# A second step of the seven-product scheme in the first product of strips 2 to 8

## The chip, the cores and the metric

The kernel runs on one core of a Trainium2 chip. The metric is the device time of one execution in microseconds (us). Five engines work from queues of their own: TensorE (PE in the profile, its weight loads PEld), VectorE (DVE), ScalarE (ACT), GpSimd (POOL) and SyncE (SP), which here issues nearly all transfers (DMA).

## The reference

```python
def _attn_ref(q, k, v, g_norm):                 # (8, 8, 576, 64) each, g_norm (64,)
    kv = np.einsum('bhsd,bhse->bhde', k, v)
    out = np.einsum('bhsd,bhde->bhse', q, kv)
    rms = np.sqrt(np.mean(out * out, axis=-1, keepdims=True) + 1e-06)
    return (out / rms * g_norm).astype(np.float32)

def _moe_ref(x, w_in, w_out):                   # x (4608, 512), w_in (512, 2048), w_out (2048, 512)
    h = x @ w_in
    r = np.maximum(h, 0.0)
    g = r * r
    return (g @ w_out).astype(np.float32)
```

The attention output, with heads side by side, is the x of the second part. Everything is fp32; the weights arrive as 64-bit words and are converted in the kernel.

## The kernel before

The 4608 rows of x are nine strips of 512 rows, numbered s = 0 to 8 here as in the code. Each strip has a first product (x @ w_in, then relu and square) and a second product (@ w_out). The attention work that makes the rows of later strips is cut into slices (`slices`, `attend`), and the main loop puts some of them between the steps of the products, spread over the first 42% of a strip's work. The order on each engine is the order in which the program's lines run (`tc.manual_schedule()`); the loop near the end of the function writes it by hand: a list `steps` per strip, one function call each, with other work hung on certain step numbers.

Both products save multiplications by the seven-product scheme for 2x2 blocks (seven products of half-size blocks in place of eight, at the price of sums of blocks). The order of the seven is `ORDER` = 1, 2, 6, 5, 7, 3, 4, and they accumulate in PSUM banks named by `BANK`: products 1, 6, 7, 4 follow each other in bank A, 5 and 3 in B, 2 in C. After products 1, 6 and 5 ScalarE copies the bank to SBUF (`snap`, L621); a result is a bank plus such a copy.

- **First product.** Strip 0 is plain (`up_first`). From strip 1 on, `up(s, g, p)` takes one step of the scheme: 4 groups g of columns by 7 products p, each of 2 x 2 matmuls of a 128x128 block of weights with 256 columns of x (L611). `combine` calls `relu_squared`: an add of bank and copy (L675) and a fused relu and square (L676) on VectorE; for the last result ScalarE does both from the bank (L680, L681). The results lie in four tiles `gq[s, 11], [12], [21], [22]`. The block sums of w_in are kept in SBUF (`w_in[..., 0:7]`, places by `A_IN`), those of x are made by `sums_x` on VectorE.
- **Second product.** From strip 1 on it takes two steps of the scheme: `down_deep(s, k, i)` runs seven outer products (`DEEP_ORDER`) of seven inner ones, `small_products`, each of four matmuls with 128 columns (L821). `leaf_sums` makes the inner sums of `gq` on VectorE, `together` adds the results, `send` stores them. The sums of w_out lie in DRAM (`w_out`, `w_deep`) and are streamed: `stream()` issues the next load into a pool of four 1 MB buffers (`stream_pool`), one call per half of an outer product, so that a load is asked for when the buffer's last user has been issued.
- **Buffers.** [...]`fpsum` holds four by tags (A twice, B, C); `apsum` holds two for keys, values and transposes ("at") and one tile of two banks for queries. `c_pool` has six buffers for the copies and the output tiles, `sum_pool` eight for sums.
- **Strip 0** also converts the weights and makes their sums; at its last step it calls `stream(2)`.

Of the kernel before, what the change touches and what calls it, by code (L numbers as in the profile page):

```python
# [20 lines left out]
def kernel(  # L21
# [50 lines left out]
    N_STRIP = N_TILE // NT  # L72
    DEEP = 1
    SQ = 32
    Q_ON_PE = 2
# [16 lines left out]
    wtmp = conv.enter_context(tc.tile_pool(name="wtmp", bufs=4))  # L92
    fpsum = ctx.enter_context(tc.tile_pool(name="fpsum", bufs=1, space=bass.MemoryType.PSUM))
    opening = ExitStack()
# [89 lines left out]

    w_deep = dram.tile([7, P, 4, FQ // 2, P], FP32, name="w_deep")

    w_out_11, w_out_21, w_out_t1 = w_first = [
# [280 lines left out]
    def first_features(p):  # L468
        t, x = x_n.pop(("first", p)), open_xt(0)
        ps = fpsum.tile([P, NT, P], FP32, name="xt_ps", tag="C")  # L470
        for n in range(NT):
            nc.tensor.transpose(ps[:, n, :], t[:, n, :], ident)
        nc.scalar.activation(x[:, :, p, :], flat(ps).rearrange("p (a t) -> p a t", t=SQ), AF.Copy, scale=g_col)
# [3 lines left out]
    def first_up(p, tiles):  # L477

        for j in tiles:
            if p == 0:  # L480
                first_sums[j] = fpsum.tile([P, STRIP], FP32, name=f"ps_{TAG_UP[j]}", tag=TAG_UP[j], bufs=2 if TAG_UP[j] == "A" else 1)
            fh, i = divmod(j, 2)
            nc.tensor.matmul(
                first_sums[j], lhsT=w_in[:, p % KH, 0, p // KH * 2 + fh, ts(i, P)], rhs=xt[0][:, :, p, :],
                start=p == 0, stop=p == NP - 1,
            )
# [115 lines left out]
    def open_bank(p):  # L602
        b = BANK[p]
        if p in (1, 5, 2):
            bank[b] = fpsum.tile([P, 2, 2 * P], FP32, name=f"ps_{b}", tag=b, bufs=2 if b == "A" else 1)
        return bank[b]
# [37 lines left out]
    def up_first(g, fh, i):  # L644

        tag = TAG_UP[2 * fh + i]
        if g == 0 and 2 * fh + i in first_sums:
            ps = first_sums.pop(2 * fh + i)
        else:
            ps = fpsum.tile([P, STRIP], FP32, name=f"ps_{tag}", tag=tag, bufs=2 if tag == "A" else 1)  # L650
            for kc in range(NP):
                nc.tensor.matmul(
                    ps, lhsT=w_in[:, kc % KH, g, kc // KH * 2 + fh, ts(i, P)], rhs=xt[0][:, :, kc, :],
                    start=kc == 0, stop=kc == NP - 1,
                )
        dest = quarters(0, g)
        for th in range(2):
            o = dest[(11, 12, 21, 22)[2 * fh + th]][:, i, :]
            nc.scalar.activation(o, ps[:, ts(th, TH)], AF.Relu)
            nc.scalar.activation(o, o, AF.Square)  # L660
# [24 lines left out]
    for p, t in zip((1, 2, 5), w_first):  # L685
        w_blk[0, p] = t.rearrange("p f (h e) -> p h f e", h=2)
    DEEP_ORDER = (4, 1, 2, 6, 5, 7, 3)
    to_stream = [(s, p) for s in range(DEEP) for p in ORDER if (s, p) not in w_blk]
    to_stream += [(s, p, n) for s in range(DEEP, N_STRIP) for p in DEEP_ORDER for n in range(2)]
    to_stream = iter(to_stream)  # L690
# [4 lines left out]
    def stream(n=1):  # L695
        for _, u in zip(range(n), to_stream):
            p = u[1]
            t = stream_pool.tile([P, 4, FQ // 2, P], FP32, name="w_blk", tag="w_blk")
            if len(u) == 2:
                w_blk[u] = t.rearrange("p (h a) f e -> p h (a f) e", h=2)  # L700
# [92 lines left out]

    def leaf_sums(s, p):
        a = gq[s, A_G[p]]
        a11, a12, a21, a22 = (a[:, ts(f, FQ // 2), ts(t, P)] for t in range(2) for f in range(2))
        s1, s2, s3, s4 = (sum_pool.tile([P, FQ // 2, P], FP32, name=f"g_s{i}", tag="sum") for i in range(4))
        leaf[p] = {1: a11, 2: a12, 3: s4, 4: a22, 5: s1, 6: s2, 7: s3}
        nc.vector.tensor_tensor(out=s1, in0=a21, in1=a22, op=ALU.add)
        minus(nc.vector, s2, s1, a11)  # L800
        minus(nc.vector, s4, a12, s2)
        minus(nc.vector, s3, a11, a21)


# [5 lines left out]
    def small_products(s, p, js):  # L810
        c = "B" if p in (4, 2, 5, 3) else "A"
        if js[0] == 1 and p not in (6, 7, 3):
            chain[c] = [
                fpsum.tile([P, 4, P], FP32, name=f"ps_{c}", tag=t, bufs=2 if t == "A" else 1)
                for t in ("AA" if c == "A" else "CB")
            ]
        for j in js:
# [34 lines left out]
    def down_deep(s, k, i):  # L852
# [28 lines left out]
        if k == 6 and s + 1 < N_STRIP:  # L881
            sums_x(s + 1)

    attend(ready[0])
    opening.close()
    apsum = ctx.enter_context(tc.tile_pool(name="apsum", bufs=2, space=bass.MemoryType.PSUM))
    for i in range(NP, NP + 2):
        convert_on_act(i)
    acted[0] = NP + 2
    for s in range(N_STRIP):  # L890
        attend(ready[s])
        if s == 0:
            steps = [(2, up_first, (g, fh, i)) for g in range(NG) for fh in range(2) for i in range(2)]
# [10 lines left out]
        for i, (w, fn, a) in enumerate(steps):  # L904
# [28 lines left out]
            if s:  # L933
                attend(ready[s] + int((goal - ready[s]) * min(done / (0.42 * total), 1)))
                if s >= DEEP and i == n_up - 3:
                    leaf_sums(s, 4)
                continue
            if i == n_up + 1:
# [8 lines left out]
            if i == n_up + 11:  # L947
                sums_x(1)
            if i == len(steps) - 1:
                stream(2)  # L950

            n = i + 1 - (n_up - 6)
# [35 lines left out]
```

## Time and profile before

| | |
|---|---|
| runs | 938.18, 933.09, 938.22 us (median 938.18) |
| profiled execution | span 932.3 us; the page lists no other time for it |
| granted TensorE clock | 0.995 |
| first product of strips 2 to 8, from the chain's stage boundaries | 54.6, 54.2, 54.7, 55.5, 54.7, 50.5, 48.4 us |
| second product of strips 1 to 8 | 43.8 us each |
| DMA | 191.48 MB, mean 205 GB/s, main queue 62.9% of 16 engines |

The page lists busy time by engine, the chain of work that ended last (followed back from the last instruction to whatever released it), groups of instructions by line with the mean time of one, and transfers. Matmuls overlap, so the mean duration of a matmul record (381 ns at L611, 275 ns at L821) is longer than the distance from one to the next; the distance is read from stretches of the chain. Some groups the text uses, with mean ns of one: L621 ScalarE copy of a bank, 586; L675 VectorE add, 680 to 690; L676, 692; L680 and L681 on ScalarE, 597 and 630; VectorE SBUF sums of 128x512, 683 to 692, and of 128x2048, 2284. Loads of 768 KB (`w_blk<-w_out`) land 5.1 us after issue, those of 1 MB 5.5 us. VectorE waited four times, 6.2 us at most, for a load of q, in strip 1 the longest.

### The profile page before, as it was taken

What the parts mean: (1) busy time and instruction counts of PE and PEld (TensorE: products, weight loads), DVE (VectorE), ACT (ScalarE), POOL (GpSimd) and SP (SyncE); (2) the same over time, 40 slices, a digit from 0 to 9 for tenths busy, and PEclk for the clock granted to TensorE, in tenths of its full rate; (3) what the DMA queues carried; (4) which work ended last, traced back from release to release, by engine and by line L of the source; (5) the groups of instructions that cost most, each with busy time, mean ns of one, the idle gap of its engine ahead of it and who ended that gap; (6) DMA issues with size and microseconds to landing.
All of it is one profiled execution on the core that took longest, in us unless ns stands there. A gap on an engine that the chain in (4) does not pass through costs nothing.

```text
span 932.3 us, 17478 instructions
## 1 busy us (share of the span) xinstructions
PE 913.8 (98%) x7070; PEld 810.1 (87%) x7070; DVE 684.3 (73%) x1195; ACT 225.9 (24%) x494; POOL 1.7 (0%) x7
## 2 busy tenths in 40 slices
PE   6999999999999999999999999999999999999998
PEld 6534788889988998899889998899889988998898
DVE  3899979379737985589648974797559855983496
ACT  3797432320022002310221022201230022002200
POOL 0000000000000000000000000000000000000000
PEclk8999999999999999999999999999999999999999
DMA  8599998828853685568564865477507731682075
GB/s 279 205 295 303 290 382 249 262 85 291 314 138 90 235 301 158 113 218 296 171 155 159 295 217 144 111 286 257 158 24 262 268 105 57 245 287 67 1 264 177
DMA packets 165728, 191.48 MB, mean 205 GB/s; under 512 B 84112, under 2 KB 137872, under 8 KB 157200
## 3 DMA queue, kind: packets, MB, share of 16 engines
q1 hardware_dynamic: 165328, 190.23, 62.9%
q8 instruction: 56, 0.92, 0.4%
q10 hardware_dynamic: 320, 0.13, 0.1%
q14 instruction: 24, 0.20, 0.1%
HBM read 159.12 MB, written 31.20 MB: 204 GB/s over the span
## 4 chain that ended last, share of the span: by engine, by line
PE 83%; DVE 7%; DMA 4%; ACT 2%; SPq 2%; issue 1%; DVEq 0%; ACTq 0%
PE ps_A L611 23%; PE ps_B L821 21%; PE ps_A L821 16%; PE ps_B L611 11%; PE ps_C L611 6%; PE kv_ps L366 2%; DVE w_t L249 2%; PE x_ps L397 2%; DMA w_out<-w_in 1%; DMA q<-in_q_dram 1%; DVE w_in L249 1%; ACT w_c L211 1%; DVE w_c L229 1%; DMA v_rest<-in_v_dram 1%; DVE gt L249 1%
## 5 line engine op out<-in xcount | busy, mean ns | idle before, releaser
L611 PE MATMUL ps_A<-x_t,w_in 128*128 128x256 f32 x768 | 183.3, 381 | 0.1
L611 PEld LDWEIGHTS ps_A<-x_t,w_in 128*128 128x128 f32 x768 | 144.4, 190 | 20.6 <-DVE gt L675 0.6
L821 PE MATMUL ps_B<-w_blk,g_s 128*128 128x128 f32 x1024 | 124.8, 275 | 0.0
L821 PEld LDWEIGHTS ps_B<-w_blk,g_s 128*128 128x128 f32 x1024 | 119.5, 192 | 0.0
L821 PE MATMUL ps_B<-w_blk,gt 128*128 128x128 f32 x768 | 96.2, 275 | 0.0
L821 PE MATMUL ps_A<-w_blk,g_s 128*128 128x128 f32 x768 | 93.6, 275 | 0.0
L821 PEld LDWEIGHTS ps_B<-w_blk,gt 128*128 128x128 f32 x768 | 91.5, 192 | 0.4
L821 PEld LDWEIGHTS ps_A<-w_blk,g_s 128*128 128x128 f32 x768 | 89.6, 192 | 0.0
L675 DVE TENSOR_TENSOR gt<-ps_A,snap 128x512 f32<-128x512 f32 x32 | 22.0, 688 | 71.0 <-PE ps_A L611 71.0
L821 PE MATMUL ps_A<-w_blk,gt 128*128 128x128 f32 x576 | 72.2, 275 | 0.0
L676 DVE SCALAR_TENSOR_TENSOR gt<-gt 128x512 f32<-128x512 f32 x96 | 66.4, 692 | 3.3
L675 DVE TENSOR_TENSOR gt<-ps_C,snap 128x512 f32<-128x512 f32 x32 | 22.1, 690 | 63.2 <-PE ps_C L611 63.2
L821 PEld LDWEIGHTS ps_A<-w_blk,gt 128*128 128x128 f32 x576 | 68.2, 192 | 0.0
L621 ACT COPY snap<-ps_A 128x512 f32<-128x512 f32 x66 | 38.7, 586 | 114.1 <-PE ps_A L611 103.0
L611 PE MATMUL ps_B<-xT,w_in 128*128 128x256 f32 x256 | 61.1, 381 | 0.4 <-ACT snap L621 0.4
L611 PE MATMUL ps_A<-xT,w_in 128*128 128x256 f32 x256 | 61.2, 382 | 0.0
L611 PE MATMUL ps_C<-xT,w_in 128*128 128x256 f32 x256 | 61.1, 381 | 0.0
L611 PE MATMUL ps_B<-x_t,w_in 128*128 128x256 f32 x256 | 61.0, 381 | 0.0
L249 DVE TENSOR_TENSOR gt<-gt 128x2048 f32<-128x2048 f32 (+1 forms) x29 | 59.7, 2063 | 0.0
L835 DVE TENSOR_TENSOR o_sb<-o_sb,ps_B 128x256 f32<-128x256 f32 (+1 forms) x128 | 49.4, 386 | 12.5 <-ACT o_sb L836 4.2
L611 PEld LDWEIGHTS ps_B<-xT,w_in 128*128 128x128 f32 x256 | 48.1, 190 | 7.5 <-ACT snap L621 0.8
L611 PEld LDWEIGHTS ps_B<-x_t,w_in 128*128 128x128 f32 x256 | 48.2, 190 | 6.7
(126 smaller groups left out, 1111.0 us busy)
## 6 DMA issues: line engine op xcount, KB each, us to landing
w_blk<-w_deep SPq DMA_DIRECT2D x56, 1024.0 KB, 5.5
w_blk<-w_out SPq DMA_DIRECT2D x56, 768.0 KB, 5.1
raw<-in_moe_w_in_dram SPq DMA_DIRECT2D x16, 512.0 KB, 5.7
raw<-in_moe_w_out_dram SPq DMA_DIRECT2D x16, 512.0 KB, 5.6
k<-in_k_dram SPq DMA_DIRECT2D x29, 256.0 KB, 2.9
v<-in_v_dram SPq DMA_DIRECT2D x29, 256.0 KB, 3.3
x_d<-x_q SPq DMA_DIRECT2D x27, 256.0 KB, 2.1
xT<-x_d SPq DMA_DIRECT2D x108, 64.0 KB, 2.0
```

The source lines that it names most:

```text
L211: nc.scalar.activation(c, high_f, AF.Abs)
L229: yield nc.vector.scalar_tensor_tensor(out=ci, in0=high, scalar=-(2**30), in1=ci, op0=ALU.bitwise_and, op1=ALU.bitwise_or)
L249: eng.tensor_tensor(out=out, in0=a, in1=b, op=ALU.subtract)
L366: nc.tensor.matmul(ps[ts(h, D)], lhsT=a, rhs=w, start=c == 0, stop=c == C)
L397: nc.tensor.matmul(ps[half, r, i, ts(p, D)], lhsT=q[row, half], rhs=kvd[b, p][row, row], start=True, stop=True)
L611: nc.tensor.matmul(bank[BANK[p]][:, i, :], lhsT=lhsT(k), rhs=rhs(k), start=p in (1, 5, 2) and i == 0 and k == 0, stop=k == n - 1, skip_gro ...
L621: nc.scalar.copy(snap[p], b)
L675: nc.vector.tensor_tensor(out=o, in0=b, in1=a, op=ALU.add)
L676: nc.vector.scalar_tensor_tensor(out=o, in0=o, scalar=0.0, in1=o, op0=ALU.max, op1=ALU.mult)
L821: nc.tensor.matmul(chain[c][x][:, i, :], lhsT=a[:, f, :], rhs=w[:, f, :], start=p not in (6, 7, 3) and j in ((1, 2) if place(s, p) is LAST ...
L835: add = lambda out, a, b: nc.vector.tensor_tensor(out=out, in0=a, in1=b, op=ALU.add)
```

## The change

From strip 2 on (`DEEP_UP = 2`) the first product takes two steps of the scheme as well. Seven outer products in the order `UP_SETS` have seven inner ones each. An inner one (`up_small`) is four matmuls of a 128x128 weight block with 128 columns of x, one for each 128-wide block of features. The outer products are staggered: a strip has 57 slots, and outer product n runs its inner product number i in slot 7n + 2i, so that two outer products alternate.

Inner results are added up by VectorE from PSUM into the copy's buffer, and GpSimd adds that into one or two of the `gq` units of the outer scheme. The fourth inner product of an outer one goes from the bank straight to `gq`. Relu and square move to ScalarE, on SBUF, two or four slots after the last addend (`relus`). Sums of x are on GpSimd: `sum_x` for the outer scheme and `leaf_x` for the inner one, the latter one outer product ahead, and for n = 0 at the end of the strip before in the place of `sums_x`.

The inner scheme needs seven forms of each of the seven weight sums. Three more per sum (`deep_sums_in`) are made on GpSimd during strip 1, stored to DRAM in `w_in_deep`, and streamed from strip 2 on: seven loads of 768 KB a strip, put into the order of `to_stream` ahead of the strip's other loads, one `stream()` call after inner product 3. One form is made in place in `w_in` once strip 1 no longer needs the original (`deep_differences_in`).

PSUM: one tag "f" with four banks takes the place of A, B and C; from strip 2 on it has five, and "at" one. The `stream(2)` at the end of strip 0 moves to four steps before the end of strip 1's first product. `leaf_sums(s, 4)` is split over two slots. Cut to its core:

```diff
+    DEEP_UP = 2
+    fpsum = psums.enter_context(tc.tile_pool(name="fpsum", bufs=4, space=bass.MemoryType.PSUM))
+    w_in_deep = dram.tile([7, P, 3, 2, WN // 2], FP32, name="w_in_deep")
...
+    UP_SETS = (1, 2, 6, 7, 5, 3, 4)
+    for s in range(DEEP, N_STRIP):
+        to_stream += [("in", s, p) for p in UP_SETS if s >= DEEP_UP]
+        to_stream += [(s, p, n) for p in DEEP_ORDER for n in range(2)]
...
         if k == 6 and s + 1 < N_STRIP:
-            sums_x(s + 1)
+            leaf_x(s + 1, 0)
...
+    def deep_sums_in(b):
+        t = stream_pool.tile([P, 4, FQ // 2, P], FP32, name="w_i", tag="w_blk")
+        s1, s2, s4 = (t[:, i].rearrange("p f e -> p (f e)").rearrange("p (g e) -> p g e", g=2) for i in range(3))
+        nc.gpsimd.tensor_tensor(out=s1, in0=w_half(b, 0, 1), in1=w_half(b, 1, 1), op=ALU.add)
+        minus(nc.gpsimd, s2, s1, w_half(b, 0, 0))
+        minus(nc.gpsimd, s4, w_half(b, 1, 0), s2)
+        nc.sync.dma_start(
+            out=w_in_deep[b].rearrange("p n g e -> p n (g e)"), in_=t[:, 0:3].rearrange("p n f e -> p n (f e)")
+        )
+    def deep_differences_in(b):
+        minus(nc.gpsimd, w_half(b, 0, 1), w_half(b, 0, 0), w_half(b, 0, 1))
...
+    def leaf_x(s, n):
+        x = operand_x(s, UP_SETS[n])
+        t = leaf_t[s, n] = sum_pool.tile([P, 4, TH // SQ // 2, SQ], FP32, name="x_l", tag="sum")
+        late = x[:, 4:8].rearrange("p a k t -> p k a t")
+        minus(nc.gpsimd, t[:, 0:2], late, x[:, :, 0].rearrange("p (h a) t -> p h a t", h=2))
+        minus(nc.gpsimd, t[:, 2], late[:, 1], t[:, 0])
+        minus(nc.gpsimd, t[:, 3], x[:, 0:4, 1], t[:, 2])
+    SUM_AT = {2: 5, 4: 6, 11: 7, 18: 4}
+    FINAL = {2: 11, 5: 22, 3: 12, 4: 21}
+    def up_slot(s, slot):
+        for n, p in enumerate(UP_SETS):
+            i, odd = divmod(slot - 7 * n, 2)
+            if not odd and 0 <= i < 7:
+                up_small(s, n, p, ORDER[i], slot)
+        if slot in SUM_AT:
+            sum_x(s, SUM_AT[slot])
+        n, at = divmod(slot, 7)
+        if at == 3 and n < 6:
+            leaf_x(s, n + 1)
+        for o in relus.pop(slot, ()):
+            nc.scalar.activation(o, o, AF.Relu)
+            nc.scalar.activation(o, o, AF.Square)
+    def up_small(s, n, p, j, slot):
...
+        for i in range(4):
...
+            nc.tensor.matmul(
+                ps[:, i, :], lhsT=w, rhs=rhs, start=j in (1, 2, 5) and i == 0, stop=True, skip_group_check=True
+            )
+        if j == 3:
+            stream()
+        if j in (1, 6, 5):
+            snap[n, j] = c_pool.tile([P, 4, P], FP32, name=f"snap{j}", tag="c")
+            nc.scalar.copy(snap[n, j], ps)
+            return
...
+        to = {1: [(12, None)], 2: [(11, 12)], 6: [(12, 12)], 7: [(21, 12)], 5: [(22, 21), (12, 12)], 3: [(12, 12)], 4: [(21, 21)]}[p]
+        if j == 4:
+            for q, before in to:
+                if before is None:
+                    nc.scalar.copy(unit(q), ps)
+                else:
+                    add(nc.vector, unit(q), ps, unit(before))
+        else:
+            other = snap.pop((n, {2: 1, 7: 5, 3: 6}[j]))
+            if p == 1:
+                add(nc.vector, unit(12), ps, other)
+            else:
+                add(nc.vector, other, ps, other)
+                for q, before in to:
+                    add(nc.gpsimd, unit(q), unit(before), other)
+        if p in FINAL:
+            relus.setdefault(slot + (2 if j == 4 else 4), []).append(unit(FINAL[p]))
...
+        if s == DEEP_UP:
+            while queried:
+                attend(slice_at[0] + 1)
+            psums.close()
+            fpsum = ctx.enter_context(tc.tile_pool(name="fpsum", bufs=5, space=bass.MemoryType.PSUM, reuse_waits="tile"))
+            apsum = ctx.enter_context(tc.tile_pool(name="apsum", bufs=1, space=bass.MemoryType.PSUM, reuse_waits="tile"))
+        if s >= DEEP_UP:
+            quarters(s, 0)
+            steps = [(0.5, up_slot, (s, slot)) for slot in range(57)]
...
+                if s == 1 and i < n_up and i % 3 == 2 and i < 21:
+                    deep_sums_in(i // 3)
+                if s == 1 and i == n_up - 4:
+                    stream(2)
+                if s == 1 and n_up <= i < n_up + 7:
+                    deep_differences_in(i - n_up)
+                if s >= DEEP_UP and i == 45:
+                    first_leaf = leaf_sums_of(s, 4)
+                if s >= DEEP_UP and i in (45, 47):
+                    next(first_leaf)
...
-            if i == len(steps) - 1:
-                stream(2)
```

## The prediction

> **What bounds the kernel now.** I read four views, in this order: busy time by engine, the chain that ended last, busy time by stage, and single instructions around the start of a strip. All times are us unless a row says ns.
>
> First the page's busy times.
>
> ```profile
> PE 913.8 (98%) x7070; PEld 810.1 (87%) x7070; DVE 684.3 (73%) x1195; ACT 225.9 (24%) x494; POOL 1.7 (0%) x7
> ```
>
> TensorE is busy nearly all the time, and GpSimd (POOL) does nothing. A busy TensorE need not be at its peak, so the second view is the chain that ended last, in order of time (start, length, what, number of instructions).
>
> ```profile
> 836.13 1.73 PE ps_A L611 x8
> 846.49 3.45 PE ps_A L611 x16
> 858.58 3.45 PE ps_A L611 x16
> 870.67 3.45 PE ps_A L611 x16
> 884.48 6.25 PE ps_B L821 x56
> 890.73 6.25 PE ps_A L821 x56
> ```
>
> This is the last strip, s = 8, which has no attention work in it. From 836.13 to 884.48 runs the first product (L611), 48.35, in a gapless chain of TensorE. Each fp32 matmul of the program appears as two instructions, so 112 matmuls on 256 columns are 224 instructions: 48.35 / 224 = 215.8 ns each. The second product (L821) takes 6.25 per 56 instructions on 128 columns: 111.6 ns each. Two levels of the seven-product scheme make 196 matmuls of 128 columns, 392 instructions. Third, the stages (length, then busy time and count by engine, clock, DMA share, GB/s).
>
> ```profile
> 347.90:402.00 54.10, 54.10 (x401) 46.22 (x401) 29.33 (x53) 14.28 (x31) 0.00 (x0) 1.00 0.53 143
> 402.00:445.80 43.80, 43.80 (x394) 43.80 (x393) 40.37 (x64) 3.10 (x9) 0.00 (x0) 1.00 0.78 278
> 836.10:884.50 48.40, 48.40 (x227) 42.61 (x226) 18.88 (x29) 10.72 (x18) 0.00 (x0) 1.00 0.15 46
> ```
>
> The first row is the first product of strip 3 with attention mixed in, the second its second product, the third the first product of strip 8. In all, TensorE is the limit, and VectorE and ScalarE have room in the first product.
>
> **What the Trainium skill says.** "GPSIMD Engine Reference", section 3.1 (elementwise accounting), gives a two-input fp32 add over 2048 elements 4497 ns on GpSimd and 2293 ns on VectorE. The trace has the VectorE half: 128x2048 takes 2284 ns and 128x512 about 690. It has no GpSimd add. "SBUF — State Buffer", section "Who interferes with whom": a VectorE instruction with two SBUF inputs and a GpSimd instruction that reads SBUF exclude each other for a whole instruction; with one SBUF input there is no conflict. No row here shows it. "TensorE: Matmul & The Clock Gate", section "Back-to-back issue gap", lets the gap grow with the columns plus a few ns; the trace agrees (215.8 against 111.6, a ratio of 1.93).
>
> **The change part by part.**
>
> *TensorE.* Seven strips lose 224 instructions at 215.8 ns (48.35) and gain 392 at 111.6 (43.75). I take 111.6 because L821 has the same shape; the moving operand's runs of 32 elements are already there in L611. Gain 4.60 a strip, 32.2 in all, all on the path.
>
> *VectorE.* Per strip it loses 12 pairs L675/L676 (12 x 1.38 = 16.6) and four sums of x (4 x 0.69), and gains 27 adds from PSUM (27 x 0.69 = 18.6): net -0.7. These adds have one SBUF input, so GpSimd doesn't block them.
>
> *ScalarE.* It loses 12 snapshots at 0.586 and four pairs at 0.597 + 0.630 (11.9), and gains 25 copies at 0.586 and 16 pairs at about 1.26 (34.8). Busy 14.3 + 22.9 = 37 of about 50: it fits, but not evenly (below).
>
> *GpSimd.* Per strip 25 operations over 512 elements and seven sets of three over 256, 128, 128. A quarter of 4497 is 1.12; I take 1.2 each and 1.4 a set, an estimate from that page. Six sets fall inside the product: 25 x 1.2 + 6 x 1.4 = 38.4, against 43.75. It fits at 88%. Lower bound 0.69 (VectorE's), upper 2.2, a doubling for software overhead.
>
> *Where GpSimd is late.* Between slots 29 and 38 of the 57 it gets nine adds and two sets, 13.6 in 8.9 of TensorE time. So the last outer product's set comes about when its third product wants it (slot 46). I take 0.3 a strip, 0 to 2.5.
>
> *Start of a strip.* Here only one outer product is under way. Product 6 accumulates on the bank that ScalarE copies after product 1; between them stands one product of 0.89, where there was one of 1.73. At the start of strip 8 that copy waits for an output DMA to free its buffer:
>
> ```profile
> 837.90 0.59 ACT L621 COPY snap<-ps_A 128x512 f32<-128x512 f32 x1 [2.36 <-DMA out_dram<-o_sb]
> ```
>
> The copy ends 2.36 after the strip's start, and two products cover 1.79, so 0.8 with the semaphores; there were four such waits in all. I take 0.5 a strip, 0 to 1.
>
> *End of a strip.* The last outer product has nothing beside it. Its product 4 waits for VectorE to read product 7's bank (0.69), which stands behind two leaf sums (2 x 0.69); these wait for ScalarE's pairs, and those for GpSimd's adds. One product (0.89) covers it, and the leaf sums have two SBUF inputs and can be held off by GpSimd for up to 1.2. I take 1.0, 0 to 4.
>
> *Strip 1.* 21 sums and seven differences on GpSimd, 28 x 1.2 = 34 of its 98, beside 12 L676 with two SBUF inputs and the leaf sums. TensorE waits for none of the new sums; what hides them is VectorE's slack (20 in the first product, 3.5 in the second). SP gets seven stores that wait for GpSimd, ahead of q, k and v loads; if they come late, VectorE stands at the q transpose (in this strip its longest such wait is 6.2 already). I take 1.5, 0 to 6.
>
> *DMA and SP.* 49 loads of 768 KB, 38.5 MB. The second product moves 278 GB/s at a share of 0.78, so 5.5 MB a strip are 15.5 of all engines, 0.29 of a first product: 0.53 + 0.29 = 0.82. Four buffers give each load several steps to land (5.1 in the page). Seven more issues a strip lie in SP's idle time, each behind a wait for a buffer that TensorE has just left. I cost them nothing; uncovered, a load would cost up to 5 a strip. The two loads no longer issued at the end of strip 0 come four steps before the second product of strip 1: no cost.
>
> *PSUM.* Five banks in turn for the first product, one for keys and values instead of two: these come 6.1 apart (364.18, 370.29) and their two copies take 0.42. Nothing.
>
> Sum: 932.3 - 32.2 + 7 x 1.8 + 1.5 = 914.2. The page gives the profiled execution no time apart from its span; the lowest run shown, 933.09, lies 0.8 above it, and the median, 938.18, lies 5.9 above. Against the median I add 5.9: **920**.
>
> **The rivals.**
>
> 1. *Everything is hidden.* For it: GpSimd may run ahead, since its sums of x wait only for buffers. Then 932.3 - 32.2 + 1 + 5.9 = 907.
> 2. *The queues couple.* ScalarE is in order; pairs that wait for GpSimd hold up the copies TensorE needs, and it has seven pairs (8.8) in slots 40 to 49 (8.9). At about 5 a strip the gain is gone: 932.3 - 32.2 + 35 + 1.5 + 5.9 = 942; at 3.5, 932.
> 3. *GpSimd becomes the bound*: slower. Its need is 31c + 1.2 a strip at c per add, and it idles some 6 at the strip's start, before the first results. The first products of strips 2 to 8 now last 372 together by the chain's stage boundaries, 53.2 each: from about c = 1.5 nothing is left. At c = 1.8 it is 7 x (31 x 1.8 + 1.2 + 6) = 441, so 938 + 69 = 1007. Against it: the page's price.
> 4. *The change doesn't do what it says*: the 128-column matmul is slower here than in L821. Nothing in the profile speaks for it; the operands come from the same kinds of tile.
>
> **How the numbers follow.** The likeliest case, 1 to 3 lost a strip, 912 to 929: 0.5. Rival 1: 0.2. Rival 2: 0.17. Rival 3: 0.12. Rival 4: 0.01. The range 903 to 937 takes in rival 1 and the better half of rival 2, and leaves out rival 3. About 1% (9.4) is what a measurement of this kernel can tell from no change. Faster by over 1%: 0.70; within: 0.17; slower: 0.13.
>
> **What would show it.** TensorE instructions in a first product 392 at about 111.6 ns, with L821 unchanged. A first product without attention of 45 to 47. GpSimd's 128x512 adds at 1.1 to 1.3, and 75 to 90% busy in that stage. Idle TensorE at the strip's ends, released by ScalarE's copy at the start and VectorE's add at the end. Adds of 1.5 or more, TensorE waiting for GpSimd's sums in mid-strip, or a DMA share near 1 would prove the forecast wrong.

## The result, and the profile after

The changed kernel takes 986.13 us (median of 982.77 to 990.47) against 937.4 for the kernel before: ratio 1.0533, 95% interval 1.0493 to 1.0572. It is 5% slower; 920 was forecast. The profiled execution spans 980.3 us, 48.0 more than before.

The page's busy times and its row of the granted clock, in 40 slices:

```profile
PE 909.0 (93%) x8246; PEld 843.2 (86%) x8246; DVE 724.3 (74%) x1195; ACT 361.2 (37%) x732; POOL 351.6 (36%) x357
...
PEclk7999998999999899989999999999998999999999
```

TensorE's busy time was to fall by 32.2 from 913.8 and fell by 4.8, and TensorE is now idle 71.3 instead of 18.5. So it lost some 27 of busy time that the number of instructions does not ask for, and 53 of waiting. Most of the 27 is a lower clock: the granted clock was 0.970 over the span instead of 0.995, about 25 of 980. VectorE is 40 busier with the same number of instructions. GpSimd is busy 36% of the span, and inside a first product 36.6 of 55.8 (strip 3) or 36.3 of 47.2 (strip 8).

Stages of strip 3 (first and second product) and the first product of strip 8 (length, busy time and count by engine, clock, DMA share, GB/s):

```profile
366.60:422.40 55.80, 51.33 (x571) 49.66 (x571) 35.42 (x60) 31.45 (x62) 36.57 (x38) 0.97 0.75 201
422.40:469.10 46.70, 45.82 (x394) 45.63 (x394) 37.67 (x57) 4.87 (x13) 7.74 (x9) 0.96 0.82 299
885.10:932.30 47.20, 44.67 (x395) 44.12 (x394) 24.75 (x36) 27.55 (x48) 36.31 (x37) 1.00 0.44 149
```

Without attention the first product became 1.2 shorter; with attention it became longer, and the second product, whose instructions were not touched, went from 43.8 to 46.7. By stage boundaries the 48.0 divide up like this (the last columns are two of the experiments):

| stages | before | after | both edits | all edits |
|---|---|---|---|---|
| start of strip 1 | 148.4 | 151.5 | 155.6 | 148.8 |
| strip 1, both products | 100.9 | 110.9 | 110.7 | 110.3 |
| first products of strips 2 to 6 | 273.6 | 296.8 | 266.7 | 277.4 |
| first products of strips 7 and 8 | 98.8 | 98.4 | 93.3 | 96.8 |
| second products of strips 2 to 7 | 262.6 | 274.8 | 276.9 | 263.3 |
| second product of strip 8, to the end | 48.0 | 48.1 | 50.2 | 48.6 |

The start of strip 1 varied between 147.9 and 155.6 in the profiles of kernels that share that part, so its 3.1 is no effect of the change. With the forecast's 32.2 in hand, 77 were lost: 46 in strips 2 to 6, 9 in strips 7 and 8, 12 in second products, 10 in strip 1.

What TensorE waits for (total, times, longest):

```profile
PE ps_A L972 <- DVE snap L983: 33.3, 14, 5.9
...
PE ps_B L615 <- ACT snap L625: 4.7, 1, 4.7
PE ps_A L833 <- DMA w_blk<-w_deep: 4.3, 2, 3.4
PE ps_A L972 <- POOL x_l L253: 3.7, 5, 1.3
```

The first row is TensorE waiting until VectorE has added up a finished inner product, so that its PSUM bank is free. Its place is the end of a first product: 28.2 of the 33.3 are seven stalls, one ahead of the last inner product of each of strips 2 to 8. VectorE's timeline at the end of strip 3's first product (start, length):

```profile
413.73 0.65 DVE L983 TENSOR_TENSOR snap<-ps_B,snap 128x512 f32<-128x512 f32 x1
414.31 1.42 DVE L812 TENSOR_TENSOR g_s<-gt 128x512 f32<-128x512 f32 x1
415.76 1.65 DVE L253 TENSOR_TENSOR g_s<-g_s,gt 128x512 f32<-128x512 f32 x1
417.34 0.68 DVE L983 TENSOR_TENSOR gt<-ps_A,gt 128x512 f32<-128x512 f32 x1
417.94 0.70 DVE L510 STREAM_TRANSPOSE x_q<-x_n 128x512 f32<-128x512 f32 x1
418.56 0.64 DVE L253 TENSOR_TENSOR g_s<-gt,g_s 128x512 f32<-128x512 f32 x1
419.13 0.68 DVE L253 TENSOR_TENSOR g_s<-gt 128x512 f32<-128x512 f32 x1
419.73 0.68 DVE L983 TENSOR_TENSOR snap<-ps_A,snap 128x512 f32<-128x512 f32 x1
```

TensorE stands from 416.96 to 420.56, for the last line. Four leaf sums (g_s) that the second product needs later and a transposition for the next strip stand ahead of it in the queue, and two of the four took 1.42 and 1.65 instead of 0.69, while GpSimd was at three sums in a row (412.67 to 416.87).

The second place is in the chain of waits, right after it (start, length, what):

```profile
413.96 5.41 DMA x_d<-x_q
...
421.71 4.92 DMA x_d<-x_q
...
428.49 5.59 DMA w_blk<-w_deep
...
434.12 3.84 PE ps_A L833 x32
```

Pieces of x for the next strip go through a DRAM buffer, `x_d`: SP stores a piece, stands until the store has landed, and issues the four loads that bring it back in its new layout. Here it does so twice. Only at 428.49 can it issue the load of `w_deep` that TensorE waits for until 434.12. The wait itself is 0.9 here and 3.4 in strip 4.

### The profile page after: what moved, and what is told of

It reads as the page before. It is cut to its first block, busy times and chain, and to the rows that moved or that the text cites. A ratio compares the mean times of both kernels' runs of the same rounds, so it can differ in the third digit from the quotient of the medians.

```text
span 980.3 us, 20838 instructions
## 1 busy us (share of the span) xinstructions
PE 909.0 (93%) x8246; PEld 843.2 (86%) x8246; DVE 724.3 (74%) x1195; ACT 361.2 (37%) x732; POOL 351.6 (36%) x357
## 4 chain that ended last, share of the span: by engine, by line
PE 61%; DVE 18%; DMA 8%; ACT 4%; issue 3%; POOL 3%; SPq 3%; DVEq 0%; ACTq 0%
PE ps_B L833 19%; PE ps_A L833 14%; PE ps_A L972 13%; PE ps_B L972 5%; PE ps_C L972 3%; POOL gt L983 3%; DVE g_s L253 2%; DMA x_d<-x_q 2%; PE kv_ps L370 2%; DVE w_t L253 1%; PE ps_A L615 1%; DVE snap L983 1%; DVE w_c L233 1%; DMA q<-in_q_dram 1%; DMA w_blk<-w_deep 1%
## 5 line engine op out<-in xcount | busy, mean ns | idle before, releaser
L983 POOL TENSOR_TENSOR gt<-gt,snap 128x512 f32<-128x512 f32 x147 | 187.3, 1300 | 148.5 <-DVE snap L983 135.7
L972 PE MATMUL ps_A<-x_l,w_in 128*128 128x128 f32 x784 | 110.9, 287 | 32.6 <-DVE snap L983 32.6
L972 PEld LDWEIGHTS ps_A<-x_l,w_in 128*128 128x128 f32 x784 | 99.9, 200 | 35.4 <-issue 29.3
L253 POOL TENSOR_TENSOR x_l<-xT 128x256 f32<-128x256 f32 x21 | 15.7, 750 | 245.2 <-PE ps_A L833 245.2
L979 ACT COPY snap<-ps_A 128x512 f32<-128x512 f32 x98 | 57.0, 581 | 92.2 <-PE ps_A L972 82.6
L956 ACT ACTIVATE gt<-gt 128x512 f32<-128x512 f32 x112 | 70.3, 628 | 32.2 <-POOL gt L983 32.0
L903 POOL TENSOR_TENSOR w_i<-w_in 128x512 f32<-128x512 f32 x7 | 9.2, 1308 | 176.7 <-DMA w_blk<-w_out 154.2
L957 ACT ACTIVATE gt<-gt 128x512 f32<-128x512 f32 x112 | 70.6, 630 | 3.6
L848 ACT COPY o_sb<-ps_B 128x128 f32<-128x128 f32 x32 | 8.5, 266 | 167.8 <-PE ps_B L833 167.8
L983 DVE TENSOR_TENSOR snap<-ps_A,snap 128x512 f32<-128x512 f32 x42 | 28.7, 683 | 45.3 <-PE ps_A L972 27.4
L972 PE MATMUL ps_A<-x_l,w_blk 128*128 128x128 f32 x392 | 53.3, 279 | 3.7 <-POOL x_l L253 3.7
```

The lines of the kernel that those rows point to most:

```text
L253: eng.tensor_tensor(out=out, in0=a, in1=b, op=ALU.subtract)
L848: yield nc.scalar.copy(q[:, 3:4], small(1))
L956: nc.scalar.activation(o, o, AF.Relu)
L972: nc.tensor.matmul(ps[:, i, :], lhsT=w, rhs=rhs, start=j in (1, 2, 5) and i == 0, stop=True, skip_group_check=True)
L979: nc.scalar.copy(snap[n, j], ps)
L983: add = lambda eng, out, a, b: eng.tensor_tensor(out=out, in0=a, in1=b, op=ALU.add)
```

## Experiments

Four theories were put against each other. **V**: at a strip's end VectorE's queue is the bound. **D** (later **B**): the bytes of the streamed sums make other loads late. **G**: GpSimd's sums are late. **S**: strip 1 loses its time because GpSimd and VectorE exclude each other. **Q**, on the order in SP's queue (SP stands at x_d, and loads that TensorE needs are queued behind), came after the first four runs, and **R**, its counterpart for strip 1, after the next four. "Both edits" is leaf sums late and loads late.

| run | median us | ratio to before, 95% interval |
|---|---|---|
| changed kernel | 986.13 | 1.0493 to 1.0572 |
| e1 leaf sums late | 976.42 | 1.0391 to 1.0454 |
| e2 strip 1's sums out | 985.3 | 1.0488 to 1.0540 |
| e3 a third of the bytes | 970.06 | 1.0328 to 1.0376 |
| e4 Newton step, one input | 983.93 | 1.0480 to 1.0540 |
| e5 as e2, one store | 986.33 | 1.0488 to 1.0604 |
| e6 loads of x_d late | 972.9 | 1.0351 to 1.0433 |
| e7 both edits | 951.33 | 1.0148 to 1.0210 |
| e8 both, a third of the bytes | 950.48 | 1.0138 to 1.0211 |
| e9 both, strip 1's sums out | 945.53 | 1.0066 to 1.0121 |
| e10 both, Newton step, one input | 949.57 | 1.0097 to 1.0167 |
| e11 both, strip 1 moved | 955.46 | 1.0168 to 1.0225 |
| e12 both, attention to the end | 978.12 | 1.0417 to 1.0471 |
| e13 both, attention early | 958.18 | 1.0199 to 1.0305 |
| e14 both, leaf sums between adds | 955.22 | 1.0180 to 1.0211 |
| e15 both, GpSimd's order in strip 1 | 951.38 | 1.0143 to 1.0189 |
| e16 all edits | 946.89 | 1.0096 to 1.0127 |
| e17 all, half sums | 938.3 | 1.0013 to 1.0053 |
| e18 kernel before, loads of x_d late | 936.36 | 0.9992 to 1.0018 |

**e1: leaf sums late.**

```diff
-                if s >= DEEP_UP and i == 45:
+                if s >= DEEP_UP and i == 53:
...
-                if s >= DEEP_UP and i in (45, 47):
+                if s >= DEEP_UP and i in (53, 55):
```

> The changed kernel, but the first leaf sums of strips 2 to 8 are issued to VectorE after slots 53 and 55 instead of 45 and 47, so behind product 3's add. Theory V (at the end of a first product, VectorE's queue is the bound: the leaf sums stand ahead of the last adds from PSUM that TensorE waits for, and are stretched by GpSimd): TensorE's waits for snap L983, 33 in all, fall below 12; the second product then waits 1 to 2 a strip for its own leaf sums; 15 to 20 us off the 986, so 966 to 971. Theory D (the streamed sums of W_in make other loads late) and theory G (GpSimd's sums come too late): no change, 982 to 990, because the adds are late for other reasons.

It came to 976.42, about 10 off instead of 15 to 20. TensorE's waits in this kernel:

```profile
PE ps_B L833 <- DVE g_s L253: 12.4, 9, 1.9
PE ps_A L833 <- DMA w_blk<-w_deep: 10.1, 4, 4.9
PE ps_A L972 <- DVE snap L983: 9.8, 7, 2.4
```

The wait for snap fell from 33.3 to 9.8, as V says, and the first products of strips 2 to 6 lost 22. But the second products of strips 3 and 4 rose from 46.7 and 47.9 to 54.6 and 56.3: the stall at the strip's end had been hiding a late load. A good part of the gain went to the next thing that was late.

**e2: strip 1 without GpSimd's sums.** The three sums in `deep_sums_in` and the difference in `deep_differences_in` go; three DMAs store raw parts instead of one that stores the sums.

```diff
-        nc.gpsimd.tensor_tensor(out=s1, in0=w_half(b, 0, 1), in1=w_half(b, 1, 1), op=ALU.add)
...
+        for n, (kc, f) in enumerate([(0, 1), (1, 1), (0, 0)]):
+            nc.sync.dma_start(
+                out=w_in_deep[b][:, n], in_=w_half(b, kc, f)
+            )
...
```

> The changed kernel without GpSimd's 21 sums and seven differences in strip 1; the stores to w_in_deep stay in place and copy raw parts of W_in, so the results of strips 2 to 8 are those of other weights. Theory S (strip 1 loses its 13 us to GpSimd and VectorE excluding each other): VectorE's w_in sums back at 0.69 from 1.65, strip 1's first product at 114 instead of 123 and its second at 44 instead of 47.6: 973. If it were the seven stores in SP's queue instead: no gain, 984 to 988.

985.3, no gain: a miss, but a confounded one. VectorE's last three sums of W_in were back at 2.02, and yet strip 1 took 112.9, with TensorE waiting 4.9 for `w_out` behind SP's store of x_d. The extra DMAs had lengthened SP's queue.

**e3: a third of the bytes.**

```diff
-                nc.sync.dma_start(out=w_blk[u][:, 0:3], in_=w_in_deep[A_IN[p]].rearrange("p n g e -> p n (g e)"))
+                nc.sync.dma_start(out=w_blk[u][:, 0:1], in_=w_in_deep[A_IN[p]][:, 0:1].rearrange("p n g e -> p n (g e)"))
...
```

> The changed kernel, but each load of further sums of W_in brings one of its three parts (256 KB instead of 768), which is used for all three products: the results of strips 2 to 8 are those of other weights. Theory D (the stream makes q, v, x and w_deep late): VectorE's waits for q fall from 22.7 to about 11, the two waits for w_deep (4.3) and the v waits (3.3) go, and with them lowered clocks in the second products: 15 to 25 us less, 961 to 971. Theories V and G: 3 to 6 us less, 980 to 983, since the ends of the strips stay as they are.

970.06, in D's range: late loads cost something. But the waits for snap stayed at 31.5. It doesn't say yet whether the bytes are the cause, or an order that smaller loads only mend in part: one `w_deep` wait of 3.0 was left.

**e4: the Newton step with one input.** The three operations of `inverse_root` become `tensor_scalar`, the second for example:

```diff
-        nc.vector.tensor_tensor(out=t, in0=t, in1=r, op=ALU.mult)
+        nc.vector.tensor_scalar(out=t, in0=t, scalar1=1.0, scalar2=1.0, op0=ALU.mult, op1=ALU.mult)
```

> The changed kernel, but the three small VectorE operations of the Newton step have one SBUF input each (same number, same shapes, the step itself is not computed, so the inverse root stays that of the first estimate). If GpSimd's exclusion of two-input operations matters here: they fall from 0.4 to 0.5 us to 0.17, VectorE's busy time falls by about 13, and 1 to 2.5 us come off each strip with attention (2 to 6) and 2 off strip 1: 972 to 979. If that time lies in VectorE's slack: 984 to 988.

983.93, not to be told from no change. The edit missed its aim, as the group of the second operation in this kernel shows (count, busy us, mean ns):

```profile
L423 DVE TENSOR_SCALAR newton<-newton 128x16 f32<-128x16 f32 x14 | 6.8, 484 | 0.5
```

With one SBUF input it is as long as with two (394 in the changed kernel), against 175 before. Whether the stretched small operations matter stays open.

**e5: as e2, one store a set.**

```diff
-        nc.gpsimd.tensor_tensor(out=s1, in0=w_half(b, 0, 1), in1=w_half(b, 1, 1), op=ALU.add)
...
+        nc.sync.dma_start(
+            out=w_in_deep[b].rearrange("p n g e -> p (n g) e"),
+            in_=w_in[:, :, :, b].rearrange("p k g e -> p (k g) e")[:, 0:6],
+        )
```

> As the kernel without GpSimd's 28 sums and differences in strip 1, but each store to w_in_deep is one DMA again (raw parts of W_in), as in the changed kernel, where the former run had three DMAs for each and SP spent 3.5 us on six of them just when x_d was to be stored; the results of strips 2 to 8 are those of other weights. Theory S (GpSimd and VectorE excluding each other costs strip 1 its time): with SP's queue as in the changed kernel, strip 1 takes 101 to 103 in all against 110.9, so 976 to 979. If SP's queue is what strip 1 waits for (the loads of its second product stand behind the waits for x_d): no gain, 983 to 988, with the second product of strip 1 still at 47 or more.

986.33: S fails by itself. Strip 1 took 111.8 without one GpSimd sum in its first product; the chain in it goes three times through x_d and then through `w_out`.

**e6: SP issues the loads of x_d three steps after their store.**

```diff
-        for f in range(4):
-            nc.sync.dma_start(...)
+        x_loads.append((now[0], load))
...
+            now[0] += w
+            loads_due(3 if s else 0)
```

`load` is the loop that was taken out; `loads_due` calls those that have waited three steps' weight. A strip's start calls all of them, and no more than three may wait.

> The changed kernel, but SP issues the four loads of each x_d three steps (some 5 us) after its store, so that it doesn't stand still until the store has landed (89.9 us in 27 waits) with the streamed loads queued behind it. Theory Q (SP's order: the first loads of w_deep and w_out of a second product are issued late because they stand behind these waits; the change took their lead away): the waits for w_deep and w_out in the second product go (4.7 in the changed kernel, 13.2 with the late leaf sums) and those for v shrink: 978 to 982 here, where the strips' ends hide part. Theory B (the bytes of the stream are the cause): no gain, 983 to 988.

972.9: 13 less, more than Q had asked for. No wait for `w_deep` is left among TensorE's, and SP's waits for x_d fell from 89.9 to 39.1.

**e7: both edits.**

> Both edits: leaf sums after slots 53 and 55, loads of x_d three steps after their store. Theory Q: with the late leaf sums alone the second products of strips 3 and 4 took 54.6 and 56.3 because loads came late; now they take 46 and the 16 us that the leaf sums were to bring are seen in full: 957 to 963. Theory B: the second products of strips 3 and 4 stay above 52, 972 to 978.

951.33, 35 less, where the two alone brought 10 and 13: each had kept the other's gain hidden. Strip 3 in this kernel:

```profile
367.60:418.60 51.00, 50.12 (x570) 48.61 (x569) 31.40 (x56) 29.15 (x59) 35.25 (x37) 1.00 0.74 201
418.60:464.40 45.80, 43.98 (x394) 43.82 (x393) 40.74 (x62) 6.92 (x16) 9.44 (x10) 1.00 0.90 326
```

TensorE is busy 50.1 of 51.0, and its clock is back at 1.00. The DMA share in the second product is 0.90, against 0.82 in the changed kernel, and TensorE waits for no load of `w_deep` or `w_out` in the whole run.

**e8: both edits and a third of the bytes.**

> Both edits, and one third of the bytes of the streamed sums of W_in (one part used for three products: the results of strips 2 to 8 are those of other weights). Theory Q: little is left for the bytes, 952 to 960, 3 to 6 below the kernel with both edits. Theory B: 16 us below it or more, as the third of the bytes brought alone.

950.48, no difference from e7: 25.7 MB less move nothing once the order is right, as Q says. The bytes are not without effect, though. In e3 the stores of x_d landed after 2.4 at the median, as against 3.7 in the changed kernel and 2.1 before, and SP stood at them 68.8 instead of 89.9. The bytes lengthen the wait, and the order puts the loads of `w_deep` and `w_out` behind it; either mended shortens the delay, as the 16 of e3 and the 13 of e6 show.

**e9: both edits, strip 1's sums out**, as in e5.

> The kernel with both edits (951), without GpSimd's 28 sums and differences in strip 1 (raw parts of W_in are stored, so the results of strips 2 to 8 are those of other weights). With SP's waits for x_d out of the way, what is left of strip 1's loss (110.7 for its two products against 100.9 before the change) is put to the test. Theory S, exclusion of GpSimd and VectorE: strip 1 falls to 101 to 103, so 942 to 944. Theory R, the seven stores and the later loads in SP's queue: strip 1 stays above 107, 948 to 952.

945.53: 5.8 less than e7, between S (8) and R (0). Strip 1 takes 106.6 (110.7 in e7), with VectorE 77.2 busy instead of 88.6. So GpSimd's sums cost some 4 to 6 there, together with the stream buffers they fill and the stores that wait for them, which e9 takes out as well; and they cost it only now that SP is out of the way. Another 5.7 above the kernel before remains.

**e10: both edits, Newton step with one input.**

> The kernel with both edits, and the three operations of the Newton step with one SBUF input each (the step is not computed). Now that leaf sums and loads no longer hide it: if the stretched small operations set the end of the first products with attention (waits for snap L993 of up to 2.3), 1 to 2 us come off strips 2 to 6 each: 942 to 947. If not, 949 to 952.

949.57; the intervals of e7 and e10 overlap, and the second operation was stretched again (415 ns). Inconclusive for the same reason.

**e11: strip 1 moved.**

```diff
-                if s == 1 and i < n_up and i % 3 == 2 and i < 21:
-                    deep_sums_in(i // 3)
+                if s == 1 and i < 24 and i % 3 == 2 and i > 2:
+                    deep_sums_in(i // 3 - 1)
+                if s == 1 and i < 27 and i % 3 == 2 and i > 5:
+                    deep_store_in(i // 3 - 2)
```

`deep_store_in` issues the store from ScalarE, `stream(2)` comes four steps earlier, and the differences become VectorE's, nearly all in strip 2.

> The kernel with both edits; the 21 sums of strip 1 begin at step 5 instead of 2, behind VectorE's last sums of W_in; their stores are issued by ScalarE three steps later instead of SP; the two streamed loads come eight steps before the second product instead of four; and the seven differences are VectorE's, in strip 2's first product. If both S and R have a part: strip 1 at 102 to 105, strip 2's first product up to 2 longer, 942 to 946. If the loss is something else: 949 to 952.

955.46, a miss. GpSimd's first sum still began 0.31 after the same VectorE sum (L264) as in the changed kernel and in e7. Its queue was empty, so it began when what it waits for was there; the profile names a load of `w_out`. To issue it three steps later in the program didn't make it start later.

**e12 and e13: where attention ends.** One number, 0.42, becomes 0.5 or 0.34 from strip 2 on:

```diff
-                attend(ready[s] + int((goal - ready[s]) * min(done / (0.42 * total), 1)))
+                attend(ready[s] + int((goal - ready[s]) * min(done / ((0.5 if s >= DEEP_UP else 0.42) * total), 1)))
```

> The kernel with both edits, but the attention work of strips 2 to 7 is spread over half of the strip's weight instead of 0.42, so to the last slots of the first product. If TensorE lacks other work at a strip's end, the waits for snap and leaf sums (2.3 + 1.9 a strip) are filled in strips 2 to 7: 10 to 15 less, 936 to 941. If VectorE's queue is what is late there, its attention operations now stand in that queue: the same or up to 10 slower, 951 to 961.

> The kernel with both edits, the attention work of strips 2 to 7 spread over 0.34 of the strip's weight instead of 0.42, so it ends ten slots earlier. Spreading it over half the weight cost 27 us. Theory V (VectorE's queue at the strip's end): the waits for snap at the end go from 2.3 to about 1 in strips 2 to 6, 1 to 2 us a strip: 941 to 946. If what counts is only that TensorE's work is spread evenly: no gain, 950 to 956.

978.12 and 958.18: worse both ways. To the end:

```profile
PE ps_A L982 <- DVE snap L993: 28.4, 7, 5.4
PE ps_B L843 <- DVE g_s L253: 14.3, 6, 6.8
```

The attention operations take the leaf sums' old place in VectorE's queue, which agrees with V. Early, snap falls from 10.4 to 5.1, but TensorE now waits 9.4 for GpSimd's x_l (2.7 in e7) and 4.8 for v (1.1): probably the work is denser where GpSimd's sums and the loads of v were just in time.

**e14: leaf sums between the adds.**

```diff
-                if s >= DEEP_UP and i in (53, 55):
+                if s >= DEEP_UP and i in (47, 52):
```

> The kernel with both edits, but the leaf sums after slots 47 and 52 instead of 53 and 55: the first two in the gap between the adds of the last two outer products, the others behind product 3's add. Theory V: the second product's wait of 1.8 for g_s goes, and its first 56 instructions return to 6.25; strips 2 to 6 may lose 1 again at the snap: 940 to 948. If the leaf sums are stretched there and hold up the adds: 952 to 960.

955.22, against V's 940 to 948. The second products did fall (strip 3: 44.1), but snap doubled from 10.4 to 20.2. Between the adds the leaf sums cost no less than behind them.

**e15: GpSimd's order in strip 1.**

```diff
+                if s == 1 and i < 17 and i % 2 == 0 and i > 2:
+                    deep_sums_in((4, 5, 6, 0, 1, 2, 3)[i // 2 - 2])
...
```

The stores are issued from ScalarE and `stream(2)` comes four steps earlier, as in e11.

> The kernel with both edits; in strip 1 GpSimd begins with the three parts of W_in that VectorE's sums finish last, so that its first sum cannot run before these are done; the stores are issued by ScalarE; the streamed loads come eight steps before the second product. Theory S: VectorE's last three sums of W_in are back at 0.69, TensorE's wait of 4.5 for snap L635 at the start of strip 1 and the half clock after it go: 943 to 946. Otherwise 949 to 956.

951.38, no gain that can be measured. In the profile the wait for snap at the start of strip 1 fell from 4.5 to 1.6, and strip 1 from 110.7 to 107.4. But VectorE's last three sums of W_in still took 4.05 (5.00 in e7, 2.02 before), beside GpSimd's, and e16 and e17, which have the same strip 1, show waits of 3.6 and 4.2 there and 110.3 and 110.2 for the strip. So the edit missed its aim, and its local effect isn't shown either.

**e16: all edits.**

> All of these: leaf sums after slots 47 and 52, loads of x_d three steps late, attention over 0.34 of the weight, GpSimd's order in strip 1. If the parts add up: 928 to 936, at or below the kernel before. If the same VectorE time is counted twice: 938 to 945.

946.89, above both ranges, the shortest of those that compute everything, and still 1.1% slower than before. No second product of strips 2 to 7 waits any more (43.9), but the first products of strips 2 to 6 are back at 277.4, more than before the change. What is left sits mostly in strip 1: the profile is 13.0 longer than before, of which strip 1 has 9.4 and all of strips 2 to 8 have 3.2.

**e17: all edits, and 12 of GpSimd's 21 sums a strip over half of their elements.**

```diff
-                    add(nc.gpsimd, unit(q), unit(before), other)
+                    n = 2 if q == before else 4
+                    add(nc.gpsimd, unit(q)[:, :n], unit(before)[:, :n], other[:, :n])
```

> The kernel with all edits (947), but those of GpSimd's sums that add in place (12 of 21 in a strip) are made over half of their elements, so the results of strips 2 to 8 are incomplete. GpSimd's need falls by some 7 of 36 a strip, most of it in the last two outer products. Theory G (GpSimd's in-order queue is what is left): the waits for x_l (9.0) and snap L997 (13.4) fall by half or more and 1.5 to 3 us a strip come off strips 2 to 6: 928 to 938. If VectorE's and ScalarE's queues with the attention work are what is left: 943 to 947.

938.3, 8.6 less and 0.3 above G's range. Snap's waits fell from 13.4 to 4.1, those for x_l left the list, and the first products of strips 2 to 6 fell by 15.6 to 261.8. The second products of strips 2 to 7 rose by 7 to 270.4, with 6.8 of waiting for `w_out`: faster first products use up the loads' lead again. So GpSimd's work is a large part of what strips 2 to 8 still pay in e16, although GpSimd is busy 38% of its span. Half sums also hold VectorE up less (busy 707.9 instead of 725.5); the run doesn't tell the two apart. Strips 2 to 8 together take 672.4 here, 683.0 in the kernel before, and strip 1 (110.2) takes most of that gain back.

**e18: the kernel before, loads of x_d late**, with the edit of e6.

> The kernel before the change, with the loads of x_d issued three steps after their store. Theory Q says that SP's 59.5 us of waiting for x_d were harmless there, because four loads of the second product had been issued long before: no change, 934 to 939. If SP's waits cost the kernel before something too: 925 to 931.

936.36 against 936.16. SP waited there too, to no harm.

## Why the prediction was wrong

The direction was wrong: 66 us above the forecast and outside its range. Two steps failed. The end of a strip was priced at 1.0, 4 at most, and cost 6.4, with the lower clock that followed. The new loads were priced at nothing; they pushed the second products' loads behind SP's waits for x_d, which cost 3.6 a strip once the end of the strip was mended. The two overlap, so they are not to be added up. Step by step, in the prediction's order:

- **TensorE, 4.60 a strip: right.** A first product has 392 instructions; in e7 strip 8's took 45.2, in e17 44.2. Rival 4 fell.
- **VectorE, -0.7 a strip: about right for its count, wrong for its length.** There are 28 adds from PSUM a strip (196 in the profile), not 27, so the count gives no change. They took 680 to 692 ns, unhindered. But busy time rose by 40: leaf sums by 18 (four rows), the Newton operations by 14, the `tensor_scalar` before them by 4, strip 1's fused relu and square by 4, sums of W_in by 3. The prediction named this exclusion for strip 1 and for the end of a strip and gave the rest no price.
- **ScalarE, 22.9 a strip: 3.6 too much.** Its busy time rose by 135.3, 19.3 a strip. A strip has 22 copies of a bank (154 in the profile), not 25, which is half of the difference.
- **GpSimd, 1.2 a sum: about right.** The profile shows 1300 ns on the mean, with starts 1.23 apart where sums stand in a row. Rival 3 began at 1.5, so GpSimd was not the bound. But "it fits at 88%" judged a queue by its sum. In e17, 15% less of it (305.2 busy instead of 357.9) brought 8.6.
- **Where GpSimd is late, 0.3 a strip: about right** for TensorE's own waits, 3.7 in all (0.5). What reaches TensorE through another queue was not priced: ScalarE waited 32.0 for GpSimd's sums, and VectorE's adds 12.0 for ScalarE. **Start of a strip, 0.5: about right**, 1.8 in all (0.3).
- **End of a strip, 1.0 (0 to 4): a step that failed by its size.** The place and the mechanism were named. The 33.3 of waiting for snap are 4.8 a strip. The clock added to it: after the stalls of 2.4 to 5.9 at six of the seven ends, 12 to 25 TensorE instructions started some 213 ns apart instead of 111.6, which cost 11.5 in all. That makes 6.4 a strip. The step counted two leaf sums and one stretched; what stood in the queue were four leaf sums and the last attention operations. e1 took 23.5 of the 33.3 away.
- **DMA and SP at nothing: a step that failed by its mechanism.** The DMA share was no limit: with the order mended, a third of the new bytes in place of all brought nothing (e8). But "each behind a wait for a buffer that TensorE has just left" looked only at what the new loads wait for, not at what they and the old ones are queued behind. Before, the first four loads of strip 3's second product went out around the start of its first (347.7), and the second began at 401.9. SP's timeline of the kernel before:

```profile
338.09 0.32 SPq L704 DMA_DIRECT2D w_blk<-w_out  x1
341.66 0.32 SPq L710 DMA_DIRECT2D w_blk<-w_deep  x1
344.34 0.32 SPq L704 DMA_DIRECT2D w_blk<-w_out  x1
...
351.71 0.37 SPq L710 DMA_DIRECT2D w_blk<-w_deep  x1
...
395.65 0.35 SPq L510 DMA_DIRECT2D x_d<-x_q  x1
```

So SP could stand at x_d to no harm (e18: no price). With seven loads of W_in taking turns in the same four buffers, those of `w_deep` and `w_out` had to be issued in the very stretch in which SP stands. The same four in the changed kernel, where the second product begins at 422.4:

```profile
400.27 1.10 SPq L714 DMA_DIRECT2D w_blk<-w_out  x1
...
413.49 0.38 SPq L720 DMA_DIRECT2D w_blk<-w_deep  x1
413.96 0.38 SPq L514 DMA_DIRECT2D x_d<-x_q  x1
...
421.23 0.39 SPq L714 DMA_DIRECT2D w_blk<-w_out  x1
421.71 0.39 SPq L514 DMA_DIRECT2D x_d<-x_q  x1
...
428.49 0.38 SPq L720 DMA_DIRECT2D w_blk<-w_deep  x1
```

Before, they were issued 64 to 50 us ahead of the product that uses them; now 22, 9 and 1 us ahead, and the last 6 us after it has begun. The prediction's own price for an uncovered load, up to 5 a strip, was the right one: from e1 to e7 the later loads of x_d brought 25, 3.6 a strip.
- **Strip 1, 1.5 (0 to 6): 10.** (Its two products took 100.9 before, not the 98 of the prediction.) Of the 10, 4 to 6 go with GpSimd's sums (e9). The first of them met three VectorE sums that stood on TensorE's path. VectorE's timeline, then GpSimd's:

```profile
156.95 4.99 DVE L253 TENSOR_TENSOR w_in<-w_in 128x512 f32<-128x512 f32 x3
```

```profile
156.54 1.50 POOL L903 TENSOR_TENSOR w_i<-w_in 128x512 f32<-128x512 f32 x1 [154.23 <-DMA w_blk<-w_out]
158.12 1.60 POOL L253 TENSOR_TENSOR w_i<-w_i,w_in 128x512 f32<-128x512 f32 x1
159.80 1.60 POOL L253 TENSOR_TENSOR w_i<-w_in,w_i 128x512 f32<-128x512 f32 x1
```

Before, the same three VectorE sums took 2.02. GpSimd's sums took 1.50 to 1.60 here and 1.26 when they next ran alone, so both were held up: the two engines take turns, instruction by instruction. "TensorE waits for none of the new sums" was true and beside the point. The rest of strip 1 is not settled. The moved `stream(2)`, "no cost", showed one: in e2, e5 and e9, where strip 1's sums no longer hid it, TensorE waited 1.7 to 4.9 for `w_out`.

Of the rivals, "the queues couple" came nearest, with 942, but the queues that the experiments show to couple were SP's and VectorE's. No run takes ScalarE's queue out by itself, so its part is open. The two losses were no sum either: alone the edits bring 10 and 13, together 35.

Two pages of the Trainium skill stand behind this. "SBUF — State Buffer", section "Who interferes with whom", says that a VectorE instruction with two SBUF inputs and a GpSimd instruction that reads SBUF shut each other out; 0.69 against 1.65 above agrees. It adds that `tensor_scalar` can take both ports as well, under conditions on its operands, so "with one SBUF input there is no conflict" left a condition out: e4's 484 ns against 175 agrees with the page. "TensorE: Matmul & The Clock Gate", section "Part 1: The HAM clock gate", says that TensorE falls to half rate after about 3.4 us without work and needs about as long to come back. The 12 to 25 instructions at 213 ns (2.6 to 5.4 us) agree with the second part. The first is only rough here: a stall of 2.4, with one of 1.3 that ended 5 us ahead of it, sufficed, and one of 3.39 in strip 4 was followed by no such stretch.

Open: 5.7 of strip 1; how much of GpSimd's part is its own time and how much VectorE's stretching; what ScalarE's queue costs; and whether the stretched small operations of attention matter. No kernel here beats the one before. In e16 the two-step first product gains 2.0 in strip 8, which has no attention, nothing in strip 7, and loses 3.8 over strips 2 to 6. In e7 it gains 6.9 there, but the leaf sums then cost the second products of strips 2 to 7 14.3.

## What to carry to other kernels

Here a load's cost was set by its place in the issuing queue. So for every transfer that loses its lead, list what the queue stands at in the new stretch, not what the transfer itself waits for. Work that is moved to GpSimd is paid for on VectorE too, in every operation with two SBUF inputs that meets it (and in `tensor_scalar`, as here), so price the pair and look first at the short stretches where TensorE waits for VectorE. When two queues are late at the same place, one mended alone shows a part of its worth, or nothing.

## What the runs showed of the hardware

- A GpSimd add of 128x512 fp32 took 1.30 us on the mean (1.23 from start to start), of 128x256 0.73 to 0.75, of 128x128 0.46 when undisturbed.
- VectorE operations of 128x16 with two SBUF inputs, and a `tensor_scalar` with one, 0.175 us before, averaged 0.37 to 0.50 with GpSimd at work, and single ones took 1.2, about as long as a GpSimd sum. The reciprocal of the same size (0.25) and the adds with a PSUM input (0.68 to 0.69) were not stretched.
- GpSimd's first sum of strip 1 began 0.31 us after the same VectorE sum whether it stood at step 2 or at step 5 of the program (e11).
- A store to DRAM that is read back made SP stand 3.3 us on the mean and 5.2 at most, 89.9 in 27 waits in the changed kernel. The store landed after 3.7 at the median there, 2.1 before and 2.4 with a third of the streamed bytes (e3).
